# Four heads a transfer: K and V laid out 128 keys of one head to a partition, with scores, softmax and P V worked by head

## The chip, the cores and the metric

The kernel runs on one core of one Trainium2 chip. The metric is the device time of one execution in microseconds (us). Before the change the median of three runs is 98.94 us (98.93 to 99.21). The profile is of one more execution.

## What is computed

One token goes through attention and an MLP that share a normalised input. Sizes: D = 1024, 32 query heads of 128 in 4 groups (one key/value head serves 8 query heads), the last W = 4096 of 65536 cached keys, F = 3584, all in bfloat16.

```python
xn = layernorm(x)
q = (xn @ wq)                                    # 32 heads x 128
k, v = k_cache[:, :, Sk - W:, :], v_cache[:, :, Sk - W:, :]
o = softmax(q @ k.T / sqrt(128)) @ v             # each query head with its group's k, v
a = o.reshape(1, 4096) @ wo
y = layernorm(xn)
b = gelu(y @ w1 + b1) @ w2 + b2
out = x + a + b                                  # 1 x 1024
```

## The kernel before, in words

With one token every product is a vector by a matrix, so the weights and caches are read once each: W1 and W2 7 MB each, wq and wo 8 MB each, the two windows of K and V 4 MB each. Five engines run their own lists of instructions and meet at semaphores; the order is written out by hand.

**The transfers.** SP issues nearly all of them into one queue, in this order: W1 (L213), K in two transfers (`load_cache`, L204), wq (L196); when the h loop has read W1, W2 into its place (L372) and V in two transfers (L204); when the q loop has read wq, wo into its place in four chunks of 20, 8, 3 and 1 rows a partition (L196). ACT's queue brings b1, x and b2. Each K or V transfer carries two of the four heads: a partition holds 64 consecutive keys of one head, 16 KB, and even and odd partitions hold the two heads. The address of the same key in the next head is 65536 x 128 x 2 bytes further.

**The order of the work.** PE computes the sums for the two layernorms, then h = y W1 in a loop of eight turns (`rolled`, "h"). ACT copies h, PE transposes it (L397), DVE and ACT take the GELU (L402 to L418). Around that DVE turns K in 32 x 32 blocks, eight transposes of 2048 elements (`turn_k`, L331): three ahead of the GELU steps, one among them, four after. PE writes a mask of -1e30 into four PSUM banks (L429) and computes q in the loop "q", eight turns, each four column tiles abreast. q is copied (L432, L434), transposed (L438), repeated over the partition quarters (L448) and copied into LB, a zeroed array that holds q's weights at diagonal places (L457 on DVE, L458 on ACT, 128 elements each).

**Scores and softmax.** 32 matmuls of 128 x 512 (L483, through `full` and `tile`, so the profile shows L339) add into the masked banks. The mask is there because a bank holds two heads' keys alternating, and a query head must see only its own. One weight load serves two matmuls. DVE takes the maximum over each half (L487); PE transposes it (L499), DVE joins it (L502), ACT spreads it (L505), PE brings it back to the partitions (L508), and ACT makes the bias (L510) and four exponentials of 512 (L513). DVE transposes each block after its exponential (L517).

**P V and the output.** PE runs the MLP's second product in the loop "w2" (seven turns of 16 matmuls), brings the sums to the rows (L524), and runs the loop "pv": four turns of eight matmuls, 64 weights wide and 512 columns each, two column tiles abreast. A row then holds four blocks of 128, of which BLK picks the one that belongs to it: one ACT copy (L545) and three multiply-adds on DVE (L548). Four products with E4 (L557) turn this into OT, the attention vector in the form that wo needs (L564). `turn_over` (L541) is a matmul whose result nobody reads; there are one before and three after these products. The loop "wo" then takes 28 of wo's 32 rows in seven turns, each when SP has seen the chunk land (L569, L570); four rows follow outside the loop. ACT copies the result (L586), and ACT and SP store it (L589).

`rolled` is a loop on PE with addresses in registers; `Track` counts an engine's marked instructions in one semaphore.

Of the kernel before, what the change touches and what calls it, by code (L numbers as in the profile page):

```python
# [10 lines left out]
D = 1024  # L11
# [16 lines left out]
NPAIR = HKV // 2  # L28
NB = 64
OUTSIDE = -1e30  # L30
# [21 lines left out]
def bass_parallel_sum__sliding_block_cached__mixer_channel_mlp__decode_kernel(  # L52
# [26 lines left out]
    s_k = sems("s_k", NPAIR)  # L79
    s_v = sems("s_v", NPAIR)  # L80
# [14 lines left out]
    SAME = sb("SAME", [128, 128], f32)  # L95
# [3 lines left out]
    BLK = sb("BLK", [128, 4], f32)  # L99
    BLI = sb("BLI", [128, 8], f32)  # L100
    PAR = sb("PAR", [2, 128], bf16)
    OUTM = sb("OUTM", [2, 512], bf16)
    oneb = sb("oneb", [128, 32], bf16)
    XBR = sb("XBR", [1, 2 * D], bf16)
# [11 lines left out]
    LB = sb("LB", [128, 8 * 144], bf16)  # L116
# [9 lines left out]
    MXP = sb("MXP", [128, 3], f32)  # L126
    MXH = sb("MXH", [1, HQ], f32)
    MXQ = sb("MXQ", [1, 4 * HQ], f32)
    BIAS = sb("BIAS", [128, 1], f32)
    SUMS = sb("SUMS", [128, 4], f32)  # L130
    SUMP = sb("SUMP", [128, 1], f32)
# [6 lines left out]
    Pb = KV[:, 0:2048]  # L138
    PT = KV[:, 2048:4096]
# [62 lines left out]
    def load_cache(dst, cache, semaphores):  # L202
        for i in range(NPAIR):
            sp.dma_start(  # L204
                dst[:, 2 * i * W:2 * (i + 1) * W],
                cache[0, 2 * i:2 * i + 2, SK - W:SK, :].rearrange("g (m b) d -> m g (b d)", m=64),
            ).then_inc(semaphores[i], 16)

    act.dma_start(B1R, b1_row.rearrange("o (c n) -> o c n", c=B1N)).then_inc(s_b1, 16)
    act.dma_start(XBR[:, 0:D], x_row).then_inc(s_xrow, 16)  # L210
    act.dma_start(XBR[:, D:2 * D], b2_row).then_inc(s_b2, 16)

# [15 lines left out]
    def product(out, a, b, ready):  # L228
# [14 lines left out]
    POOL.mark(pool.memset(PAR[:, :], 0.0))  # L243
    fill(PAR[:, :].rearrange("k (e g r) -> k e g r", g=2, r=REP), [[0, 8], [1, 2], [0, REP]], 0, -1)
    POOL.mark(pool.memset(OUTM[:, :], OUTSIDE))
    C["mask"] = fill(OUTM[:, :].rearrange("k (s g) -> k s g", g=2), [[0, 256], [1, 2]], 0, -1, value=0.0)
    C["vec"] = POOL.mark(pool.memset(VEC[:, :], 0.0))
    POOL.mark(pool.memset(BLI[:, :], 1.0))
    fill(BLI[:, :].rearrange("p (i q) -> p i q", i=NPAIR), [[-64, NPAIR], [-16, 4]], 0, 1, op=ALU.is_ge, value=0.0)
    fill(BLI[:, :].rearrange("p (i q) -> p i q", i=NPAIR), [[64, NPAIR], [16, 4]], 15, -1, op=ALU.is_ge, value=0.0)  # L250
    pool.wait_ge(POOL.sem, POOL.cnt)
    POOL.mark(pool.tensor_tensor(out=BLK[:, :], in0=BLI[:, 0:4], in1=BLI[:, 4:8], op=ALU.add))
# [5 lines left out]
    POOL.mark(pool.tensor_tensor(out=HD[:, 0:64], in0=identf[:, 0:64], in1=identf[:, 64:128], op=ALU.add))  # L258
    pool.wait_ge(POOL.sem, POOL.cnt)
    POOL.mark(pool.tensor_tensor(  # L260
        out=SAME[:, :].rearrange("p (h b) -> p h b", b=4), in0=HD[:, 0:32].unsqueeze(2).to_broadcast([128, HQ, 4]),
        in1=HD[:, 32:64].unsqueeze(2).to_broadcast([128, HQ, 4]), op=ALU.add))
    parts = identf[:, :].rearrange("p (i q h) -> p i q h", i=NPAIR, q=4)
    POOL.mark(pool.tensor_tensor(out=HD[:, 64:128].rearrange("p (i q h) -> p i q h", i=NPAIR, q=2),
                                 in0=parts[:, :, 0:2, :], in1=parts[:, :, 2:4, :], op=ALU.add))
    pool.wait_ge(POOL.sem, POOL.cnt)
    HD4 = HD[:, 64:128].rearrange("p (i q h) -> p i q h", i=NPAIR, q=2)
    for i in range(NPAIR):
        C["consts"] = POOL.mark(pool.tensor_tensor(
            out=E4[:, :].rearrange("p (q r) -> p q r", r=129)[:, :, 64 * i:64 * i + 64:4],  # L270
            in0=HD4[:, i, 0, :].unsqueeze(1).to_broadcast([128, 4, 16]),
            in1=HD4[:, i, 1, :].unsqueeze(1).to_broadcast([128, 4, 16]), op=ALU.add))

# [52 lines left out]
    def turn_k(n):  # L326
        if n % 4 == 0:
            dve.wait_ge(s_k[n // 4], 16)
        else:
            dve.wait_ge(DVE.sem, DVE.cnt)  # L330
        C["kd"] = DVE.mark(dve.transpose(  # L331
            out=KD4[:, n], in_=KR[:, n * 2048:(n + 1) * 2048].rearrange("p (b e s) -> p b e s", b=16, e=4)))
# [47 lines left out]
    for n in range(3):  # L380
        turn_k(n)

# [26 lines left out]
    turn_k(3)  # L409
# [12 lines left out]
    for n in range(4, 8):  # L422
        turn_k(n)
# [3 lines left out]
    pe.wait_ge(POOL.sem, C["mask"])  # L427
    for n in range(4):
        tile(PS[:, n * 512:(n + 1) * 512], PAR[:, :], OUTM[:, :], (32, 128), (0, 0), n == 0, True)  # L429
# [20 lines left out]
    LB8 = LB[:, :].rearrange("p (e x) -> p e x", x=144)  # L450
    for eng, track, qs in ((dve, DVE, (0, 1)), (act, ACT, (2, 3))):
        eng.wait_ge(PE.sem, C["rep"])
        eng.wait_ge(POOL.sem, C["lb"])
        for q in qs:
            dst = LB8[32 * q:32 * q + 32, :, 32 * q:32 * q + 16]
            src = PS[32 * q:32 * q + 32, 6 * 512:6 * 512 + 128].rearrange("p (e h) -> p e h", e=8)
            C["lb", q] = track.mark(dve.tensor_copy(dst, src) if eng is dve  # L457
                                    else act.activation(out=dst, in_=src, func=ACTF.Copy))  # L458
# [19 lines left out]
    for half in range(2):  # L478
        for i in range(NPAIR):
            for e in range(4):  # L480
                for n in range(2 * half, 2 * half + 2):
                    at = (i * 4 + n) * 2048 + e * 512
                    last = full(PS[:, n * 512:(n + 1) * 512], LB[:, e * 288 + i * 128:e * 288 + i * 128 + 128],  # L483
                                KD[:, at:at + 512], n % 2 == 0)
        C["sc"] = PE.mark(last)
        dve.wait_ge(PE.sem, C["sc"])
        C["mx", half] = DVE.mark(dve.tensor_reduce(out=MXP[:, half:half + 1], in_=PS[:, half * 1024:(half + 1) * 1024], axis=AX.X, op=ALU.max))  # L487
# [4 lines left out]
    for a in range(4):  # L492
        for i in range(2):
            src = XBR[0:1, i * D + a * 256:i * D + (a + 1) * 256]
            tile(quad[a], oneb[0:1, :], src, (32, 32), (0, 32 * a), i == 0, i == 0)

    for half in range(2):
        pe.wait_ge(DVE.sem, C["mx", half])
        C["mxT"] = PE.mark(pe.matmul(PS[0:1, 6 * 512 + 256 + 128 * half:6 * 512 + 384 + 128 * half], lhsT=MXP[:, half:half + 1],  # L499
                                     rhs=identf[:, :], is_transpose=True))  # L500
    dve.wait_ge(PE.sem, C["mxT"])
    DVE.mark(dve.tensor_reduce(out=MXH[:, :], in_=PS[0:1, 6 * 512 + 256:7 * 512].rearrange("o (a h) -> o h a", a=8),  # L502
                               axis=AX.X, op=ALU.max))
    act.wait_ge(DVE.sem, DVE.cnt)
    C["mxh"] = ACT.mark(act.activation(out=MXQ[:, :].rearrange("o (q h) -> o q h", q=4),  # L505
                                       in_=MXH[:, :].unsqueeze(1).to_broadcast([1, 4, HQ]), func=ACTF.Copy))
    pe.wait_ge(ACT.sem, C["mxh"])
    C["mxb"] = PE.mark(pe.matmul(PS[:, 6 * 512 + 128:6 * 512 + 129], lhsT=MXQ[:, :], rhs=identf[0:1, 0:1]))  # L508
    act.wait_ge(PE.sem, C["mxb"])
    C["bias"] = ACT.mark(act.activation(out=BIAS[:, :], in_=PS[:, 6 * 512 + 128:6 * 512 + 129], func=ACTF.Copy, scale=-SCALE))  # L510
    act.wait_ge(ACT.sem, C["bias"])
    for n in range(4):
        C["exp"] = ACT.mark(act.activation(  # L513
            out=Pb[:, n * 512:(n + 1) * 512], in_=PS[:, n * 512:(n + 1) * 512], func=ACTF.Exp,
            bias=BIAS[:, :], scale=SCALE, accum_out=SUMS[:, n:n + 1]))
        dve.wait_ge(ACT.sem, C["exp"])
        C["tr", n] = DVE.mark(dve.transpose(  # L517
            out=PT.rearrange("p (i c h) -> p c i h", i=NPAIR, h=16)[:, 16 * n:16 * n + 16],
            in_=Pb[:, n * 512:(n + 1) * 512].rearrange("p (c i h) -> p c i h", i=NPAIR, h=16)))
    C["tot"] = DVE.mark(dve.tensor_reduce(out=SUMP[:, :], in_=SUMS[:, :], axis=AX.X, op=ALU.add))  # L520
    pe.wait_ge(s_w2, 16)
    steps("w2", W2, FC)
    pe.wait_ge(DVE.sem, C["tot"])
    C["rows"] = PE.mark(pe.matmul(PS[:, 5 * 512:5 * 512 + 1], lhsT=SAME[:, :], rhs=SUMP[:, :]))  # L524
    pe.wait_ge(DVE.sem, C["zo"])
    for sem in s_v:
        pe.wait_ge(sem, 16)

    def pv_rows(ws, vs):
        for r in range(8):  # L530
            i = r % 2
            last = tile(PS[64 * i:64 * i + 64, 4 * 512:5 * 512], vs[r], ws[r], (128, 64), (0, 64 * i))
        C["pv"] = PE.mark_loop(last, 4)

    rolled("pv", 4, (
        (lambda o: [V[:, bass.ds(o + i * 2 * W + j * 512, 512)] for j in range(4) for i in range(NPAIR)], 2048, False),
        (lambda o: [PT[:, bass.ds(o + i * 1024 + j * 64, 64)] for j in range(4) for i in range(NPAIR)], 256, True)),
# [9 lines left out]
    for c in range(1, 4):  # L547
# [3 lines left out]
        if c < 3:  # L551
# [69 lines left out]
```

## Time and profile before

| What | Number | Where |
|---|---|---|
| median of three runs | 98.94 us | the times |
| profiled execution | 99.1 us | the times |
| its span, first to last instruction | 97.8 us | the page |
| mean granted TensorE clock | 0.826 of full | the cores' view |
| bytes from HBM | 39.86 MB, 407 GB/s over the span | the page, part 3 |
| busy: PE, PEld, DVE, ACT, POOL | 48.0, 18.6, 31.7, 9.6, 10.9 us | the page, part 1 |
| scores: first matmul | 58.82 us | the timeline |
| end of the four exponentials | 73.3 us | the timeline |
| P V, 32 matmuls | 77.14 to 80.8 us | the timeline |
| first matmul of the wo loop | 88.76 us | the timeline |
| wo's last chunk lands | 95.73 us | the chain |

Times inside the execution count from the span's start. The profile's engines are PE (matmul), PEld (weight load, which overlaps PE), DVE, ACT, POOL and SP. A group of instructions is a line of the program, the engine, the operation, output and input tiles, the shape and the count, then busy time, mean and the idle time before it with what ended that idle time. "KV" is the one array that holds K as loaded, K turned, the weights P before and after their transposes, and V; "WW" holds W1, then W2, and wq, then wo; "PS" is PSUM. A transfer's time to landing counts from its issue on SP, not from its first byte.

The granted clock, in the 40 slices of the page, is full until about 32 us, half until about 54, and changes several times after.

### The profile page before, as it was taken

How to read it: one execution, taken by the hardware profiler on the slowest of the kernel's cores; microseconds unless marked ns; L12 is line 12 of the kernel's file. 1: busy time of each engine (PE TensorE's matmuls, PEld its weight loads, DVE VectorE, ACT ScalarE, POOL GpSimd, SP SyncE). 2: the span in 40 equal slices, each digit the busy share in tenths (PEclk: the TensorE clock that was granted, in tenths of full speed). 3: DMA queues.
4: the chain of work that ended last, by engine and by line, in shares of the span. 5: the costliest groups of instructions: out<-in, count | busy, mean ns of one | idle time of the engine just before them, and what ended most of it. 6: DMA issues, size and time to landing. Idle time of an engine off the chain costs nothing.

```text
span 97.8 us, 1231 instructions
## 1 busy us (share of the span) xinstructions
PE 48.0 (49%) x501; PEld 18.6 (19%) x415; DVE 31.7 (32%) x42; ACT 9.6 (10%) x23; POOL 10.9 (11%) x34
## 2 busy tenths in 40 slices
PE   0000022649720700000069939998479897926962
PEld 0000022213110000000012122121235544503530
DVE  0000003280699999994000050053282004100000
ACT  0500000140220000000000040000390001000001
POOL 2000001489980000000000000000000000000000
PEclk9999999999999555555555795899975999997599
DMA  9598888999999999999898889959999899799970
GB/s 375 234 519 375 376 375 376 415 435 429 429 569 455 482 429 509 429 429 455 382 422 375 375 375 422 610 221 429 435 429 563 352 452 486 318 415 429 394 316 1
DMA packets 1628, 39.86 MB, mean 407 GB/s; under 512 B 214, under 2 KB 218, under 8 KB 476
## 3 DMA queue, kind: packets, MB, share of 16 engines
q1 hardware_dynamic: 1588, 39.85, 95.4%
q10 hardware_dynamic: 40, 0.01, 0.1%
HBM read 39.86 MB, written 0.00 MB: 407 GB/s over the span
## 4 chain that ended last, share of the span: by engine, by line
DMA 87%; PE 7%; SPq 3%; issue 1%; ACT 0%
DMA WW<-in_A_wq_dram 48%; DMA WW<-in_A_wo_dram 39%; PE PS L339 7%; SPq L204 1%; SPq L196 1%; SPq L213 0%; ACT ORow L586 0%; SPq L375 0%
## 5 line engine op out<-in xcount | busy, mean ns | idle before, releaser
L331 DVE STREAM_TRANSPOSE KV<-KV 128x2048 bf16<-128x2048 bf16 x8 | 18.5, 2311 | 3.4 <-DMA KV<-in_A_k_cache_dram 3.2
L339 PE MATMUL PS<-WW,XNTb 128*32 x64 | 6.3, 580 | 15.4 <-SPq L375 15.4
L339 PE MATMUL PS<-WW,VEC 128*32 (+1 forms) x240 | 11.5, 345 | 4.6 <-SPq L569 3.1
L339 PE MATMUL PS<-KV,LB 128*128 128x512 bf16 x32 | 8.7, 438 | 0.7 <-DVE LB L457 0.7
L339 PEld LDWEIGHTS PS<-WW,VEC 128*32 (+1 forms) x236 | 6.1, 114 | 9.9 <-issue 8.9
L294 PE MATMUL PS<-oneb,XBR 1*128 1x1 bf16 x8 | 0.6, 194 | 14.0 <-DMA XBR<-in_A_x_dram 14.0
L339 PE MATMUL PS<-WW,YTb 128*32 x56 | 5.4, 519 | 1.5 <-DMA WW<-in_B_w_dram 1.5
L339 PEld LDWEIGHTS PS<-WW,XNTb 128*32 x32 | 1.3, 124 | 21.6 <-issue 21.6
L487 DVE TENSOR_REDUCE MXP<-PS 128x1 f32<-128x1024 f32 x2 | 2.4, 1224 | 7.6 <-PE PS L339 7.6
L297 DVE COPY XT<-PS 128x8 f32<-128x8 f32 x1 | 0.2, 167 | 14.6 <-PE PS L294 14.6
L434 DVE CAST Hs<-PS 128x512 bf16<-128x512 f32 x1 | 0.7, 692 | 11.0 <-PE PS L339 11.0
L339 PE MATMUL PS<-OUTM,PAR 2*128 2x512 bf16 x4 | 1.9, 615 | 4.4 <-DVE HT L402 4.4
L541 PE MATMUL PS<-E,identf 128*128 128x512 f32 x8 | 3.9, 616 | 0.0
L339 PE MATMUL PS<-KV 128*64 x32 | 3.6, 380 | 0.3 <-issue 0.3
L548 DVE SCALAR_TENSOR_TENSOR OD<-PS,BLK,OD 128x128 f32<-128x128 f32 x3 | 1.1, 350 | 7.3 <-ACT OD L545 7.2
L517 DVE STREAM_TRANSPOSE KV<-KV 128x512 bf16<-128x512 bf16 x4 | 2.7, 712 | 1.8 <-ACT KV L513 1.8
L294 PEld LDWEIGHTS PS<-oneb,XBR 1*128 1x128 bf16 x8 | 0.6, 159 | 13.9 <-issue 13.9
L339 PEld LDWEIGHTS PS<-KV,LB 128*128 128x128 bf16 x16 | 1.8, 111 | 7.0 <-issue 6.2
L432 ACT ACTIVATE Hs<-PS 128x512 bf16<-128x512 f32 x1 | 0.6, 597 | 23.0 <-PE PS L339 23.0
L513 ACT ACTIVATE KV<-PS,BIAS 128x512 bf16<-128x512 f32 x4 | 2.7, 685 | 0.0
L339 PEld LDWEIGHTS PS<-WW,YTb 128*32 x32 | 1.6, 112 | 5.6 <-issue 5.2
L220 POOL TENSOR_SCALAR_AFFINE_SELECT OUTM<-OUTM 2x512 bf16<-2x512 bf16 x1 | 2.3, 2302 | 0.1
(93 smaller groups left out, 37.3 us busy)
## 6 DMA issues: line engine op xcount, KB each, us to landing
WW<-in_B_w_dram SPq DMA_DIRECT2D x2, 7168.0 KB, 29.8
WW<-in_A_wo_dram SPq DMA_DIRECT2D x1, 5120.0 KB, 32.2
KV<-in_A_k_cache_dram SPq DMA_DIRECT2D x2, 2048.0 KB, 26.0
KV<-in_A_v_cache_dram SPq DMA_DIRECT2D x2, 2048.0 KB, 46.7
WW<-in_A_wo_dram SPq DMA_DIRECT2D x1, 2048.0 KB, 36.7
WW<-in_A_wo_dram SPq DMA_DIRECT2D x1, 768.0 KB, 38.1
WW<-in_A_wo_dram SPq DMA_DIRECT2D x1, 256.0 KB, 38.2
KV<-in_B_b_dram ACTq DMA_DIRECT2D x1, 7.0 KB, 9.0
```

The costliest lines, as they stand in the source:

```text
L196: sp.dma_start(dst[:, c0 * width:(c0 + n) * width].rearrange("p (c n) -> p c n", c=n), src[:, c0:c0 + n, :],).then_inc(semaphores[j], 16)
L204: sp.dma_start(dst[:, 2 * i * W:2 * (i + 1) * W], cache[0, 2 * i:2 * i + 2, SK - W:SK, :].rearrange("g (m b) d -> m g (b d)", m=64),).then ...
L220: return POOL.mark(pool.affine_select(out=out, in_=out, pattern=pattern, compare_op=op, fill=value, base=base, channel_multiplier=step))
L294: last = pe.matmul(xt[:, r:r + 1], lhsT=XBR[0:1, r:D:KC], rhs=oneb[0:1, 0:1])
L331: C["kd"] = DVE.mark(dve.transpose(out=KD4[:, n], in_=KR[:, n * 2048:(n + 1) * 2048].rearrange("p (b e s) -> p b e s", b=16, e=4)))
L339: return pe.add_instruction(mybir.InstMatmult(name=nc.get_next_instruction_name(), engine=pe.engine, ins=[lowered(rhs, False), lowered(lhs ...
L434: C["d_qs"] = DVE.mark(dve.tensor_copy(Qs[:, 512:1024], PS[:, 7 * 512:8 * 512]))
L487: C["mx", half] = DVE.mark(dve.tensor_reduce(out=MXP[:, half:half + 1], in_=PS[:, half * 1024:(half + 1) * 1024], axis=AX.X, op=ALU.max))
L513: C["exp"] = ACT.mark(act.activation(out=Pb[:, n * 512:(n + 1) * 512], in_=PS[:, n * 512:(n + 1) * 512], func=ACTF.Exp, bias=BIAS[:, :], s ...
L517: C["tr", n] = DVE.mark(dve.transpose(out=PT.rearrange("p (i c h) -> p c i h", i=NPAIR, h=16)[:, 16 * n:16 * n + 16], in_=Pb[:, n * 512:(n ...
L541: pe.matmul(PS[:, 3 * 512:4 * 512], lhsT=identf[:, :], rhs=E4[:, 0:512])
L548: C["d_od"] = DVE.mark(dve.scalar_tensor_tensor(out=OD[:, :], in0=PS[:, 4 * 512 + 128 * c:4 * 512 + 128 * c + 128], scalar=BLK[:, c:c + 1] ...
```

## The change

K and V are loaded in one transfer each. A partition now holds 128 consecutive keys of one head, 32 KB, and four neighbouring partitions hold the four heads (MB = 32 instead of m = 64). This changes what follows:

- One semaphore for K, one for V. All eight K transposes stand after the GELU steps on DVE. They write the same places.
- Scores go by head. A head's keys lie four elements (8 bytes) apart in a turned block, and 32 matmuls of 128 x 512 take them so, each with its own weights: a window of LB, which grows from 1152 to 2176 columns and takes q twice. The mask, its matmuls and its POOL instructions go.
- The maximum, its transpose, join, spread and bias are done twice, for heads 0 and 1 and for 2 and 3, and stand between the score matmuls of the later heads. Four exponentials write every fourth element.
- After the last exponential DVE transposes twice 1024 elements. Then the weights are copied four times, each time with the rows of one head kept and the others zeroed by the column GM[:, g]: the first half by four ACT copies, the second by four DVE multiplies, 512 elements each.
- The sums' weights (SUMX) are made by POOL after the exponentials.
- P V is 64 matmuls of 256 columns in eight turns, instead of 32 of 512 in four. A row holds two blocks of 128 instead of four: one multiply-add instead of three.
- One `turn_over` after the E4 products instead of three.
- b2 and x stand in two partitions of XBR, so four matmuls of K = 2 add them instead of eight of K = 1.

The core of the diff:

```diff
-NPAIR = HKV // 2
-NB = 64
+MB = 32
+NB = W // MB // 2
+WIN = 136
...
     def load_cache(dst, cache, semaphore):
-        for i in range(NPAIR):
-            sp.dma_start(
-                dst[:, 2 * i * W:2 * (i + 1) * W],
-                cache[0, 2 * i:2 * i + 2, SK - W:SK, :].rearrange("g (m b) d -> m g (b d)", m=64),
-            ).then_inc(semaphores[i], 16)
+        sp.dma_start(
+            dst[:, :], cache[0, :, SK - W:SK, :].rearrange("g (m b) d -> m g (b d)", m=MB),
+        ).then_inc(semaphore, 16)
...
     def turn_k(n):
-        if n % 4 == 0:
-            dve.wait_ge(s_k[n // 4], 16)
+        if n == 0:
+            dve.wait_ge(s_k, 16)
...
-    for n in range(3):
-        turn_k(n)
...
-    turn_k(3)
...
-    for n in range(4, 8):
+    for n in range(8):
         turn_k(n)
...
-    for n in range(4):
-        tile(PS[:, n * 512:(n + 1) * 512], PAR[:, :], OUTM[:, :], (32, 128), (0, 0), n == 0, True)
     q_rows(KC)
...
+    def scores(g):
+        for c in range(2):
             for e in range(4):
-                for n in range(2 * half, 2 * half + 2):
+                at = (e * HKV + g) * WIN + 8 - 8 * c
+                last = full(PS[:, g * 512:(g + 1) * 512], LB[:, at:at + 128],
+                            KG[:, e, g, 4 * c:4 * c + 4, :], True, c + e == 0)
...
+    scores(0)
+    scores(1)
+    take_max(0)
+    scores(2)
+    turn_max(0)
+    join_max(0)
+    scores(3)
+    take_max(1)
+    spread_max(0)
+    weigh(0)
...
+    turn_max(1)
+    join_max(1)
+    spread_max(1)
+    weigh(1)
...
+        C["tr", half] = DVE.mark(dve.transpose(out=PT[:, half * 1024:(half + 1) * 1024], in_=Pb[:, half * 1024:(half + 1) * 1024]))
+    for half, eng, track in ((0, act, ACT), (1, dve, DVE)):
+        eng.wait_ge(DVE.sem, C["tr", half])
+        for g in range(HKV):
+            dst, src = PG4[:, g, half * HB:half * HB + HB], PT4[:, half * HB:half * HB + HB]
+            C["pg", half] = track.mark(
+                dve.tensor_scalar(out=dst, in0=src, scalar1=GM[:, g:g + 1], scalar2=None, op0=ALU.mult) if half
+                else act.activation(out=dst, in_=src, func=ACTF.Copy, scale=GM[:, g:g + 1]))
     pe.wait_ge(s_w2, 16)
     steps("w2", W2, FC)
+    pool.wait_ge(ACT.sem, C["exp"])
+    C["sumx"] = POOL.mark(pool.tensor_tensor(
...
-    rolled("pv", 4, (
+    rolled("pv", NB // 8, (
+        (lambda o: [VC[:, :, bass.ds(o + r * DH, DH)] for r in range(8)], 8 * DH, False),
+        (lambda o: [PG[:, bass.ds(o + r * 64, 64)] for r in range(8)], 512, True)),
         pv_rows)
...
-    for c in range(1, 4):
+    for c in range(1, 2):
...
-    for _ in range(3):
-        turn_over()
+    turn_over()
```

## The prediction

> **What bounds the kernel now.** I read the chain that ended last first, then the transfers, then the timeline of the second half.
>
> ```profile
> DMA 87%; PE 7%; SPq 3%; issue 1%; ACT 0%
> DMA WW<-in_A_wq_dram 48%; DMA WW<-in_A_wo_dram 39%; PE PS L339 7%; SPq L204 1%; SPq L196 1%; SPq L213 0%; ACT ORow L586 0%; SPq L375 0%
> ...
> KV<-in_A_k_cache_dram SPq DMA_DIRECT2D x2, 2048.0 KB, 26.0
> KV<-in_A_v_cache_dram SPq DMA_DIRECT2D x2, 2048.0 KB, 46.7
> WW<-in_A_wo_dram SPq DMA_DIRECT2D x1, 2048.0 KB, 36.7
> WW<-in_A_wo_dram SPq DMA_DIRECT2D x1, 768.0 KB, 38.1
> WW<-in_A_wo_dram SPq DMA_DIRECT2D x1, 256.0 KB, 38.2
> ```
>
> These are parts 4 and 6 of the page (the last column is us from issue to landing). 87% of the span is one stream of transfers. All weights and both caches go through SP's queue, W1, K, wq, W2, V, wo, and each issue stands in the queue long before its turn: V is issued at 26.7 and 27.4 and lands on average 46.7 later, so the bytes ahead of it set its time, not the issue. 39.86 MB at 407 GB/s over the span leaves little idle.
>
> ```profile
> 57.44 0.04 issue
> 57.48 38.25 DMA WW<-in_A_wo_dram
> 95.73 0.04 issue
> 95.77 0.29 PE PS L339 x4
> 96.06 0.02 issue
> 96.09 0.38 ACT ORow L586
> ```
>
> This is the end of the same chain, in order of time (start, us, what). The last byte of wo lands at 95.73; only four matmuls, one copy and the two stores follow. The time is therefore the stream's end plus a fixed 2.1 us to the span's 97.8, plus 1.3 us outside it: the profiled run took 99.1, 0.16 over the median of 98.94. I forecast a difference and put it on the median.
>
> How much can the rest move before it counts? The timeline:
>
> ```profile
> 58.82 1.44 PE L339 MATMUL PS<-KV,LB 128*128 128x512 bf16 x3 [0.74 <-DVE LB L457]
> ...
> 64.06 1.22 DVE L487 TENSOR_REDUCE MXP<-PS 128x1 f32<-128x1024 f32 x1 [5.36 <-PE PS L339]
> ...
> 76.44 0.38 PE L524 MATMUL PS<-SUMP,SAME 128*128 128x1 f32 x2
> ...
> 77.14 3.65 PE L339 MATMUL PS<-KV 128*64 x32 [0.33 <-issue]
> ...
> 83.60 0.39 DVE L564 TENSOR_SCALAR VEC<-PS,REC 128x64 bf16<-128x64 f32 x1 [1.10 <-PE PS L557]
> ...
> 88.76 0.62 PE L339 MATMUL PS<-WW,VEC 128*32 x16 [2.54 <-SPq L569]
> ```
>
> The attention vector OT is done at 83.99 (83.60 + 0.39), but the wo loop starts at 88.76, released by SP when the first 20 rows of wo land. PE waits once more, 0.59 us at 93.67, again for wo. So the attention chain has 4.77 us to 88.76 and 0.59 more in the loop: about **5.3 us of cover** before a later OT moves the end.
>
> **The change, part by part.**
>
> *The stream.* The bytes stay. K becomes one issue instead of two, V likewise, and a partition's contiguous run grows from 16 KB to 32 KB. The price of a run comes from pace: the 2048 KB chunk of wo (16 KB a partition, as K and V have now) lands 4.9 us after the chunk ahead (SP was released at 88.3 and 93.2). wq, 8192 KB in 64 KB runs, takes from K's last landing to its own: issues at 1.26 and 1.92 plus twice 26.0 make 55.2 for both K landings; the first released the transposes at 25.2, so the second is at 30.0, and wq lands at 49.44. That is 19.4 us, or 4.85 per 2048 KB. K and V together, 8192 KB, can gain at most 4 x 4.9 - 19.4 = 0.2 us and, if run length does nothing, 0. Sixteen engines carry 128 rows a transfer, so K and V cost each of them 32 runs now, 16 after and would cost 8 at wq's length: 16 of 24 runs saved, 0.2 x 16/24 = **-0.13 us**. I take this. The two issues that go (0.61 to 0.69 us each in the chain's start) free SP, but SP is far ahead and nothing waits there.
>
> [...]
>
> *K's transposes.* They now wait for all of K (30.0, not 25.2) and stand behind the GELU steps on DVE. The transposes of the h row are done at 28.1; the steps on DVE and ACT are 0.22, 0.19, 0.19, 0.23, 0.14, 0.33 and 0.32 with gaps, so DVE is free at about 30. Its last step waits for POOL's constants, now at 29.1: POOL loses the mask (0.19 + 0.41 + 0.51 + 2.30) and gains about 1 us of memset of LB, so these come earlier. Then 8 x 2.34 = 18.7 us: done at 48.8. What is queued behind on DVE is the q copy at 56.1. Cover 7.3 us; cost 0. The four mask matmuls (1.9 us at 32.5) go from a stretch in which PE waits for wq: 0.
>
> *Scores.* The q copies into LB double their elements: 281 ns at 128 elements and 692 at 512 (the Hs cast) give 418, twice, +0.27 us. The scores stay 32 matmuls of 512 columns, each with its own weight load (PEld 0.1 us, beside the 0.22 us that a matmul takes where the clock is full; 16 of them already lie hidden). The keys are now read 8 bytes apart. The nearest row is the h loop's, whose operand is read in 8-byte pieces 56 bytes apart: between 24.5 and 26.3, at the full clock, 26 matmuls begin that run four abreast, so four take 1.8/6.5 = 0.28 us, the tail included; a contiguous score matmul takes 0.216. I take 0; the other end is a read at half pace, +5.2 us for the 24 that run at the full clock.
>
> *Softmax.* Two chains instead of one. By head 0 and 1: scores to 64.3, max 1.23 to 65.6, the third head's scores to 66.05, transpose, last scores to 68.1 while DVE and ACT join the max (0.41, 0.31), spread 0.38, bias 0.17, two exps of 0.67 to 70.1. By 2 and 3: max to 69.4, transpose, join, spread and bias to 71.2, exps to 72.7. Before they ended at 73.3. PE enters w2 at 71.15, 0.55 late, because it stands in the second max chain; w2 takes 5.85 as before, to 77.0.
>
> *Weights.* DVE transposes twice 1024 elements: between 712 (512) and 2311 (2048) that is 1.25 each, 72.7 to 75.2. Four ACT copies of 512 (0.60 by the Hs row) end at 76.5; four DVE multiplies lie between 0.14 (28 elements) and 0.69 (512 elements from PSUM) each: 75.8 to 78.0. w2 and the sums (0.38 + 0.7 as now) hold PE until 77.7 anyway, so P V starts at 77.7, or 78.2 at the upper end.
>
> *P V and after.* 64 matmuls of 256 columns instead of 32 of 512: the same columns, twice the weight loads and loop turns. At w2's pace (16 pairs in 0.86) 64 pairs take 3.45; at the q transposes' 78 ns a pair, 5.0; now 3.65. I take 3.8, to 81.5. Two of three multiply-adds go (350 each and a wait): OD at 82.35, four products 1.08, OT step: **OT at 83.9**, against 83.99 now. The ends of these terms: 83.5 (P V at 3.45) and 91.3 (all upper ends at once: 5.2 scores, 0.5 weights, 1.2 P V, 0.5 for strided writes and loop turns that no row prices). Two turn-overs go, 1.7 us of PE; PE then idles from 84.6 to 88.76. If this lowers the granted clock there, nothing follows: the loop's turns are 0.86 apart both where it is 0.5 (74.15, 75.02) and where it is full (70.59 to 72.38 in two).
>
> Sum: -0.13 from the stream, 0 from all that lies under it. 98.94 - 0.13 = **98.8** (the profiled time by the same sum 99.0).
>
> **The rivals.**
>
> *The attention chain outgrows its cover* (slower). Place: the strided key read in the 32 score matmuls, with the weight masks and the P V loads behind it. It decides once OT is later than 89.3, 5.3 us over now. Half pace alone (+5.2) just fits; with the upper ends of the other terms OT is at 91.3, 2.0 late, and the time 101. For it: these reads and products are in no row. Against: the h loop's pace. 0.09.
>
> *Four heads alternating slow the source* (slower). Neighbouring partitions' rows lie a head apart, 65536 x 128 x 2 B = 16 MB, now over four heads. If K and V fall to the slowest pace that a chunk shows, 768 KB in 1.9 us or 5.05 per 2048 KB, that is 4 x 0.15 = +0.6 us: 99.5. Against: two heads already alternate at full pace. 0.07.
> [...]
>
> *Merging is worth more than runs* (faster): a transfer has a cost of its own beside its runs. The 768 KB chunk lands 1.9 us after the one ahead, 0.1 above pace; if that is a cost of each transfer, two fewer give 0.2, with the full 0.2 of the runs 0.4: 98.5. Against: the 256 KB chunk is not late by as much. 0.08.
>
> **How the numbers follow.** Forecast 0.76 (own range 98.65 to 99.2, the spread of the runs shown, 98.93 to 99.21, being 0.28), slower 0.16, faster 0.08. About 0.3%, 0.3 us, is what a measurement of this kernel can tell from no change. The range takes in the source rival and the faster one, 98.5 to 99.5, and leaves the chain's 101 out.
>
> **What would show it.** Right: wo's last landing still ends the chain, near 95.6; K lands once near 30, transposes end near 49; OT between 83 and 85, and PE waits for SP before the wo loop. Wrong: PE, DVE or ACT in place of wo at the chain's end, score matmuls over 0.4 us apart at the full clock, or V landing after 76.2.

## The result and the profile after

The changed kernel takes **103.02 us** in the median of six runs (102.51 to 104.22), against 98.97 for the kernel before (98.93 to 99.21). The ratio is 1.0407, with a 95% interval of 1.0359 to 1.0455; it leaves out the longest of the six, a slow execution. The profiled execution took 102.51 us, the shortest of the six, with a span of 101.1 and a mean granted clock of 0.865. The forecast of 98.8 was wrong; the first rival, the attention chain that outgrows its cover, is what happened.

First the page of the changed kernel: the chain's shares, three groups of instructions, and the two transfers.

```profile
DMA 84%; PE 10%; issue 2%; SPq 1%; ACT 0%
...
L333 PE MATMUL PS<-KV,LB 128*128 128x512 bf16 x32 | 14.7, 630 | 1.0 <-DVE LB L445 1.0
...
L333 PE MATMUL PS<-KV 128*64 x64 | 5.0, 278 | 2.3 <-issue 1.2
...
L510 ACT ACTIVATE KV<-PS,BIAS 128x512 bf16<-128x512 f32 x4 | 5.2, 1400 | 0.1
...
KV<-in_A_k_cache_dram SPq DMA_DIRECT2D x1, 4096.0 KB, 28.7
KV<-in_A_v_cache_dram SPq DMA_DIRECT2D x1, 4096.0 KB, 49.0
```

The same groups on the page of the kernel before:

```profile
L339 PE MATMUL PS<-KV,LB 128*128 128x512 bf16 x32 | 8.7, 438 | 0.7 <-DVE LB L457 0.7
...
L513 ACT ACTIVATE KV<-PS,BIAS 128x512 bf16<-128x512 f32 x4 | 2.7, 685 | 0.0
```

The same 32 score matmuls of 512 columns were busy for 8.7 us before and are for 14.7 now. The four exponentials take 1400 ns each instead of 685. Nothing in their shapes tells why: an access pattern is not printed, only its count of elements. The two transfers are as forecast.

The end of the chain, in order of time:

```profile
55.13 37.78 DMA WW<-in_A_wo_dram
...
92.93 0.02 SPq L600
...
93.03 0.62 PE PS L333 x16
...
98.25 1.10 PE PS L333 x33
...
99.37 0.38 ACT ORow L617
```

It still names a transfer of wo, but not its last chunk: that landed at 95.44, and PE had 3.9 us left after it. The whole loop of wo stands behind 93.03. The transfer named is wo's second chunk, which was released at 92.93, by chance just as PE came to the loop; the first turn needs only the first chunk, which landed at 88.00. That it held nothing is shown by the run with 16 pairs a turn (below), where the loop starts at 91.95, before that chunk. What ended last before 93.03 is the attention vector, with one turn-over on PE beside it, which ends at 92.85; the reordered run (below) has no turn-over there and starts the loop just as long after its vector, 0.67 us against 0.68 here, so it is the vector that counts. The timeline:

```profile
57.67 11.01 PE L333 MATMUL PS<-KV,LB 128*128 128x512 bf16 x24 [0.96 <-DVE LB L445]
...
68.63 3.77 PE L333 MATMUL PS<-KV,LB 128*128 128x512 bf16 x8
...
72.44 1.23 DVE L488 TENSOR_REDUCE MXP<-PS 128x2 f32<-128x1024 f32 x1 [3.33 <-PE PS L333]
...
82.20 0.38 PE L555 MATMUL PS<-onesf,SUMX 128*128 128x1 f32 x2
...
83.67 0.63 PE L333 MATMUL PS<-KV 128*64 x8 [1.09 <-ACT KV L547]
...
84.51 0.63 PE L333 MATMUL PS<-KV 128*64 x8 [0.21 <-issue]
...
91.95 0.40 DVE L595 TENSOR_SCALAR VEC<-PS,REC 128x64 bf16<-128x64 f32 x1 [1.10 <-PE PS L589]
```

OT is done at 92.35 (91.95 + 0.40), against 83.99 before. By stretches, in us:

| Stretch | Before | After | Moves OT by |
|---|---|---|---|
| first score matmul | 58.82 | 57.67 | -1.15 |
| scores | 8.66 | 14.74 | **+6.08** |
| scores' end to w2's start | 3.12 | 3.95 | +0.83 |
| w2 | 5.91 | 5.91 | 0 |
| w2's end to P V | 0.63 | 1.40 | +0.77 |
| P V | 3.65 | 6.24 | **+2.59** |
| P V to OT | 3.20 | 2.44 | -0.76 |
| OT | 83.99 | 92.35 | +8.36 |

The first row is hardly a gain of the change: the q loop was granted a clock of 0.73 in this execution and 0.57 in that of before, and ended 1.36 earlier (0.2 of it because wq had landed sooner, 49.25 against 49.44). The second row also holds some clock: before, the first eight score matmuls ran at half the clock (0.50 granted from 59.2 to 61.9), 0.427 us apart.

### The profile page after: what moved, and what is told of

It reads as the page before. It is cut to its first block, busy times and chain, and to the rows that moved or that the text cites. A ratio compares the mean times of both kernels' runs of the same rounds, so it can differ in the third digit from the quotient of the medians.

```text
span 101.1 us, 1321 instructions
## 1 busy us (share of the span) xinstructions
PE 49.6 (49%) x523; PEld 20.5 (20%) x460; DVE 32.4 (32%) x42; ACT 15.1 (15%) x29; POOL 9.1 (9%) x33
## 4 chain that ended last, share of the span: by engine, by line
DMA 84%; PE 10%; issue 2%; SPq 1%; ACT 0%
DMA WW<-in_A_wq_dram 47%; DMA WW<-in_A_wo_dram 37%; PE PS L333 10%; SPq L203 1%; SPq L211 0%; ACT ORow L617 0%; SPq L196 0%; SPq L369 0%; SPq L600 0%
## 5 line engine op out<-in xcount | busy, mean ns | idle before, releaser
L333 PE MATMUL PS<-WW,XNTb 128*32 x64 | 5.2, 481 | 21.3 <-SPq L369 21.3
L333 PE MATMUL PS<-KV,LB 128*128 128x512 bf16 x32 | 14.7, 630 | 1.0 <-DVE LB L445 1.0
L333 PE MATMUL PS<-WW,VEC 128*32 (+1 forms) x240 | 10.2, 309 | 2.5 <-issue 2.3
L333 PE MATMUL PS<-KV 128*64 x64 | 5.0, 278 | 2.3 <-issue 1.2
L488 DVE TENSOR_REDUCE MXP<-PS 128x2 f32<-128x1024 f32 x2 | 2.4, 1224 | 10.8 <-PE PS L333 10.8
L333 PEld LDWEIGHTS PS<-KV,LB 128*128 128x128 bf16 x32 | 3.6, 116 | 10.8 <-issue 9.7
L510 ACT ACTIVATE KV<-PS,BIAS 128x512 bf16<-128x512 f32 x4 | 5.2, 1400 | 0.1
L540 DVE STREAM_TRANSPOSE KV<-KV 128x1024 bf16<-128x1024 bf16 x2 | 2.4, 1224 | 4.6 <-ACT KV L510 4.6
L333 PEld LDWEIGHTS PS<-KV 128*64 x64 | 2.9, 109 | 4.2 <-issue 4.2
L547 ACT ACTIVATE KV<-KV,GM 128x512 bf16<-128x512 bf16 x4 | 2.6, 710 | 1.3 <-DVE KV L540 1.3
```

The lines of the kernel that those rows point to most:

```text
L333: return pe.add_instruction(mybir.InstMatmult(name=nc.get_next_instruction_name(), engine=pe.engine, ins=[lowered(rhs, False), lowered(lhs ...
L488: C["mx", half] = DVE.mark(dve.tensor_reduce(out=MXP[:, 2 * half:2 * half + 2], in_=PS[:, half * 1024:(half + 1) * 1024].rearrange("p (g x ...
L510: C["exp"] = ACT.mark(act.activation(out=Pb.rearrange("p (x g) -> p g x", g=HKV)[:, g, :], in_=PS[:, g * 512:(g + 1) * 512], func=ACTF.Exp ...
L540: C["tr", half] = DVE.mark(dve.transpose(out=PT[:, half * 1024:(half + 1) * 1024], in_=Pb[:, half * 1024:(half + 1) * 1024]))
L547: else act.activation(out=dst, in_=src, func=ACTF.Copy, scale=GM[:, g:g + 1]))
```

## The experiments

The theory: keys that lie 8 bytes apart make the score matmuls slow, and exponentials that write 8 bytes apart and a P V loop with twice the turns add to it; with OT past its cover, PE's chain sets the time. The rivals: the loss is in the weight loads, which no longer serve two matmuls each; or in the transfers, with four heads alternating; or in P V alone.

**Keys contiguous.** In the changed kernel each score matmul reads 512 neighbours. These are other keys, so the scores are not the reference's.

```diff
-                            KG[:, e, g, 4 * c:4 * c + 4, :], True, c + e == 0)
+                            KD[:, ((g * 2 + c) * 4 + e) * 512:((g * 2 + c) * 4 + e) * 512 + 512], True, c + e == 0)
```

> The changed kernel, but each of the 32 score matmuls reads 512 neighbouring columns of K instead of every fourth (so the scores are of other keys than they should be); weights, their 32 loads, the number of matmuls and all else stay. Theory A, the 8-byte step of the moving operand sets the pace (0.45 us per matmul at either clock): the scores fall from 14.7 to 7-9 us, OT comes near 86, wo's landing ends the chain again, 98.6 to 98.9 us. Rival B, the weight load that every score matmul now has: scores stay at 14.7, OT at 92, time 102.5 to 104. Rival C, the order of max, join and spread between the heads' scores: the scores fall but OT does not come before 90, time over 100.

Measured: 99.2 us, ratio 0.9999 (0.9983 to 1.0014); the kernel before took 99.22 beside it. The timeline of this run:

```profile
58.32 5.35 PE L333 MATMUL PS<-KV,LB 128*128 128x512 bf16 x24 [0.96 <-DVE LB L445]
...
85.17 0.39 DVE L595 TENSOR_SCALAR VEC<-PS,REC 128x64 bf16<-128x64 f32 x1 [1.10 <-PE PS L589]
...
88.55 4.11 PE L333 MATMUL PS<-WW,VEC 128*32 x80 [2.48 <-SPq L600]
```

24 matmuls take 5.35 us instead of 11.01, each still with its own weights. OT comes at 85.56 and PE waits 2.48 us for wo: OT is inside its cover again, and the whole loss is gone, though exponentials (1.40 us) and P V (6.23) are as slow as they were.

**A load for each matmul**, in the kernel before.

```diff
-                                KD[:, at:at + 512], n % 2 == 0)
+                                KD[:, at:at + 512], True)
```

> The kernel before, with a weight load for each of the 32 score matmuls instead of each second one (the same weights again, so the same result). Theory A: the loads lie under the matmuls, scores stay at 8.7 us, time 99.0 as before. Rival B, the loads cost what the changed kernel lost: scores near 14.7 us, OT near 90, time 99.5 to 100.

Measured: ratio 1.0006 (0.9991 to 1.0021). Scores take 7.07 us, 0.216 a matmul, which is the pace at the full clock, for all 32. The 32 loads (6.60 us) lie beside the matmuls; the first rival falls.

**The stride alone**, in the kernel before: the score matmuls read every fourth element (other keys than the reference's).

```diff
-                                KD[:, at:at + 512], n % 2 == 0)
+                                KD[:, i * 8192 + e * 2048:i * 8192 + e * 2048 + 2048:4], n % 2 == 0)
```

> The kernel before, with its score matmuls reading every fourth of 2048 columns (so other keys than they should) and nothing else changed. Theory A: 32 x 0.45 = 14.5 us instead of 8.7, OT near 89.8, about half a us past its cover (84.0 + 5.8 against 89.3): ratio 1.002 to 1.012. If the cover of the prediction was too large, the ratio is over 1.02; if the matmuls' pace alone made the change slow, 1.04.

Measured: ratio 1.0192 (1.0140 to 1.0243), more than the 1.002 to 1.012 expected. Scores take 14.6 us. The timeline around OT:

```profile
88.88 2.82 PE L541 MATMUL PS<-E,identf 128*128 128x512 f32 x6
...
89.08 0.39 DVE L564 TENSOR_SCALAR VEC<-PS,REC 128x64 bf16<-128x64 f32 x1 [1.10 <-PE PS L557]
...
91.63 0.62 PE L339 MATMUL PS<-WW,VEC 128*32 x16
```

OT is done at 89.47, but the wo loop starts at 91.63: three turn-overs (six records, 2.82 us) stand ahead of it in PE's queue. In the changed kernel there is one.

**Merged transfers alone**: the kernel before with K and V in one transfer each, laid out as after the change (what lies in a row is then not what the rest of this kernel expects, so its output differs).

```diff
-        for i in range(NPAIR):
...
+        sp.dma_start(
+            dst[:, :], cache[0, :, SK - W:SK, :].rearrange("g (m b) d -> m g (b d)", m=32),
+        ).then_inc(semaphores[0], 16)
...
```

> The kernel before, with K and V in one transfer each in the changed kernel's layout (32 KB a partition, four heads alternating) and nothing else changed (so the scores and P V take rows of other heads than they should). This is the stream's term alone: forecast -0.13 us, from 0 to -0.2, ratio 0.998 to 1.000; K and V each land 0.07 us sooner after what is ahead of them. Rival, four heads alternating slow the source: K and V land later, ratio 1.006. Rival, a transfer has a cost of its own beside its runs: ratio 0.996 or less.

Measured: ratio 0.9977 (0.9954 to 1.0000), that is -0.23 us with an interval from -0.46 to 0. The landings tell it more finely. K lands 9.72 us after W1 and V 9.71 after W2; before it was 9.79 for each. In the changed kernel it is 9.74 and 9.71 (20.17 to 29.91, 66.17 to 75.88). So the merge brings each cache some 0.07 us, as forecast: four heads alternating slow nothing, and the 0.4 us of the third rival is too much. (Before, the 256 KB chunk of wo landed 0.62 us after the one ahead, at 95.73 after 95.11; at wq's 4.85 per 2048 KB it would be 0.61.) Whether the longer runs or the transfers that went bring it is not shown, since one edit changes both.

**Exponentials written contiguously**, in the changed kernel. The weights then reach P V in another order, so the output differs.

```diff
-                out=Pb.rearrange("p (x g) -> p g x", g=HKV)[:, g, :], ...
+                out=Pb[:, g * 512:(g + 1) * 512], ...
```

> The changed kernel, but each exponential writes 512 neighbouring elements instead of every fourth (so the weights stand in another order than P V takes them). Theory A2, the 8-byte step of the write doubles the exponential (1400 ns against 685): 0.69 each again; the first two stand ahead of PE's way into w2 and bring P V 1.0 us forward, the last two lie under w2: time about 102, 1.0 less than the changed kernel. Rival: the exponentials are slow for another reason (their bias by column, or contention with the transposes on DVE): they stay at 1.4 and the time at 103.

Measured: 102.24 us, ratio 1.0276 (1.0219 to 1.0332); an exponential takes 0.69 us. The step is worth 1.3% by the ratios and 0.8 us by the medians while OT sets the end; in the profiled executions the way from the first score matmul to OT is 1.63 us shorter.

**P V with 16 pairs a turn**, in the changed kernel: four turns of 16 loads and matmuls instead of eight of 8, the same matmuls.

```diff
-    rolled("pv", NB // 8, (
-        (lambda o: [VC[:, :, bass.ds(o + r * DH, DH)] for r in range(8)], 8 * DH, False),
+    rolled("pv", NB // 16, (
+        (lambda o: [VC[:, :, bass.ds(o + r * DH, DH)] for r in range(16)], 16 * DH, False),
...
```

> The changed kernel, P V in four turns of 16 matmuls instead of eight turns of 8; the same 64 matmuls and weight loads. Theory D, a turn of a PE loop costs some 0.8 us however little is in it (P V's turns are 0.78-0.83 apart with 0.43 us of columns in them, w2's 0.86 with twice as many matmuls): P V takes 3.5 to 5 us instead of 6.2 and the time falls by 1.2 to 2.6 us, ratio to before 1.015 to 1.028. Rival, the 64 weight loads of 64 columns set the pace (0.1 us each): P V stays at 6.2 and the ratio at 1.04.

Measured: 101.98 us, ratio 1.0297 (1.0246 to 1.0348). The weight loads in the timeline of this run:

```profile
84.31 0.80 PEld L333 LDWEIGHTS PS<-KV 128*64 x16 [1.68 <-issue]
...
85.48 0.80 PEld L333 LDWEIGHTS PS<-KV 128*64 x16 [0.36 <-issue]
...
86.65 0.80 PEld L333 LDWEIGHTS PS<-KV 128*64 x16 [0.37 <-issue]
```

A turn of 16 takes 1.12 to 1.17 us, one of 8 took 0.78 to 0.83. The starts of the matmuls show where this goes. Inside a turn of either kernel two matmuls, which run abreast (3 to 9 ns apart), start every 0.109 us (0.13 for the first two); their 256 columns cost that by themselves (256 x 0.42 ns, 0.216 us for 512). The rest is a gap at the end of a turn: **0.32 to 0.38 us** in turns of 8, 0.23 to 0.27 in turns of 16. In the kernel before there is none: with 512 columns a matmul, two start every 0.215 us straight through all four turns, 0.86 us of columns a turn. What PE does in the gap is not shown; in the program the loop's registers are set there.

P V takes 4.52 us instead of 6.24, but starts 0.65 later. Of this, 0.30 stands between the end of ACT's copies and the loop (1.19 us against 0.89), where the program sets twice as many registers. The run gains 1.04 us in the median, a little less than the 1.2 us that were the least expected.

**Four strides in one run.** In the changed kernel the four heads' keys are read at steps of 1, 2, 4 and 8 elements, and the exponentials write at the same steps (not the reference's data).

```diff
-                            KG[:, e, g, 4 * c:4 * c + 4, :], True, c + e == 0)
+                            KD[:, c * 8192 + e * 1024:c * 8192 + e * 1024 + 512 * 2 ** g:2 ** g], True, c + e == 0)
...
```

> The changed kernel as a gauge: the four heads' scores read K at steps of 1, 2, 4 and 8 elements (2, 4, 8, 16 bytes), and the four exponentials write at these steps (so neither the keys nor the weights are the right ones). Theory A: score matmuls 0.216 us apart at full clock at step 1, 0.45 at step 4, and the step decides, not the clock; if a line of 16 bytes is what is fetched, 0.22 at step 2 and 0.9 at step 8; if any step over one element halves the pace, 0.45 at 2, 4 and 8. The exponentials 0.69 at step 1 and 1.4 at step 4; steps 2 and 8 tell which it is there. Rival B: 0.45 at all four steps.

Measured, 512 columns: matmuls 0.216, 0.226, 0.453 and 0.900 us apart, the first three at the full clock (L478 behind them took 0.29 us, as in the changed kernel where the granted clock was 1.00). Exponentials 0.69, 0.82, 1.41 and 2.54 us. The loads of neighbouring matmuls at step 4 and at step 8, then the exponentials at 2, 4 and 8:

```profile
63.27 0.12 PEld L333 LDWEIGHTS PS<-KV,LB 128*128 128x128 bf16 x1 [0.34 <-issue]
...
63.73 0.12 PEld L333 LDWEIGHTS PS<-KV,LB 128*128 128x128 bf16 x1 [0.34 <-issue]
...
67.89 0.12 PEld L333 LDWEIGHTS PS<-KV,LB 128*128 128x128 bf16 x1 [0.78 <-issue]
...
68.79 0.12 PEld L333 LDWEIGHTS PS<-KV,LB 128*128 128x128 bf16 x1 [0.78 <-issue]
...
74.00 0.82 ACT L510 ACTIVATE KV<-PS,BIAS 128x512 bf16<-128x512 f32 x1
...
75.92 1.41 ACT L510 ACTIVATE KV<-PS,BIAS 128x512 bf16<-128x512 f32 x1
...
77.13 2.54 ACT L510 ACTIVATE KV<-PS,BIAS 128x512 bf16<-128x512 f32 x1
```

It doubles from 2 to 4 and from 4 to 8, so it goes by something that a read touches. Bytes spanned and lines of 16 bytes give the same answer up to here; wider steps tell them apart.

**Steps of 3, 6, 16 and 32** (again other data).

```diff
+                            KD[:, 0:1 + 511 * (3, 6, 16, 32)[g]:(3, 6, 16, 32)[g]], True, c + e == 0)
```

> The changed kernel as a second gauge: the four heads' score matmuls read 512 elements of K at steps of 3, 6, 16 and 32 elements (6, 12, 32, 64 bytes; other keys than they should be). If a line of 16 bytes costs 1.76 ns to fetch, as steps 2, 4 and 8 of the first gauge fit (128, 256 and 512 lines in 0.226, 0.453 and 0.90 us), the matmuls are 0.34, 0.68, 0.90 and 0.90 us apart. If the bytes spanned count instead, 0.34, 0.68, 1.8 and 3.6. If the number of elements out of order counts, the same for all four.

Measured: 0.340, 0.676, 0.917 and 0.858 us apart. From a step of 8 on it no longer grows, as lines of 16 bytes want it: every element is then in a line of its own. The clock was half at the end of step 32 (the two L483 behind it took 0.58 us together, in the changed kernel at the full clock 0.38). The price of a line does not go by the clock: the changed kernel's score matmuls are 0.453 us apart both where the granted clock was 0.50 (59.4 to 61.7) and where it was full (68.6 to 72.3). The last matmuls at step 3 were 0.427 us apart, which is the pace of 512 contiguous columns in the kernel before at half the clock.

**Pieces**: the four heads read 4 of every 8 elements, 4 of 16, 2 of 8 and 2 of 16 (other data).

```diff
+                            KD[:, 0:512 // (4, 4, 2, 2)[g] * (8, 16, 8, 16)[g]].rearrange("p (a w) -> p a w", w=(8, 16, 8, 16)[g])[:, :, 0:(4, 4, 2, 2)[g]], True, c + e == 0)
```

> The changed kernel as a third gauge: the four heads' score matmuls read 512 elements in pieces: four neighbours of each 8, four of each 16, two of each 8, two of each 16 elements (other keys than they should be). If a line of 16 bytes costs 1.76 ns, whatever lies between, the lines are 128, 128, 256 and 256 and the matmuls 0.226, 0.226, 0.453 and 0.453 us apart at the full clock; this is also why the h loop's reads of four neighbours of each 28, from which the prediction took its price, were at full pace and said nothing of single elements 8 bytes apart. If the first two are slower than 0.25, the line is not the unit and the h loop's pace has another reason.

The windows of one head each (us; busy time of PE and PEld, with counts; granted clock; share of the transfers; GB/s):

```profile
58.60:60.40 1.80, 1.80 (x9) 0.76 (x10) 1.00 1.18 510
60.40:62.20 1.80, 1.80 (x9) 0.76 (x8) 1.00 1.18 510
62.20:65.80 3.60, 3.60 (x9) 0.79 (x7) 1.00 0.91 391
65.80:69.60 3.80, 3.80 (x9) 0.92 (x8) 1.00 0.98 423
```

Eight matmuls take 1.8 us with pieces of four neighbours and 3.6 to 3.8 with pieces of two, whether the pieces lie 16 or 32 bytes apart (starts 0.226 and 0.229, then 0.452 and 0.461 us apart, all at the full clock). 512 columns touch 128 lines of 16 bytes in the first two heads and 256 in the last two. **A line costs about 1.76 ns** (0.453 / 256; 0.900 / 512), a column at the full clock 0.42 ns (0.216 / 512). Four elements a line are thus nearly hidden (1.69 ns of columns to a line) and two are not (0.84).

**Turned by head**: DVE writes the turned K so that each head's keys are neighbours, in 32 transposes of 512 elements instead of eight of 2048; the result is unchanged.

```diff
-    KD4 = KD.rearrange("p (n e b s) -> p n b e s", n=8, e=4, b=16)
+    KD4 = KD.rearrange("p (n e g b m) -> p n e b m g", n=8, e=4, g=HKV, b=16)
...
```

> The changed kernel, but DVE puts each head's keys side by side when it turns K (each of the 8 transposes cut in four by quarter of the head's width, its 32 outputs going to four places), so that the score matmuls read neighbouring columns; the result is the reference's. Theory A: scores at 0.216 us apart, OT near 87, wo's landing ends the chain, ratio 0.997 to 1.001. What can spoil it: 32 transposes of 512 at 712 ns are 22.8 us, done at 53, before q; if DVE's scattered writes double them, they end near 76, hold up the q copy behind them by 20 us and the time is near 120.

Measured: 146.39 us, ratio 1.4769, worse than the 120 that were expected at worst. The group of transposes:

```profile
L327 DVE STREAM_TRANSPOSE KV<-KV 128x512 bf16<-128x512 bf16 x32 | 74.3, 2598 | 0.2
```

The last eight score matmuls take 1.89 us, 0.216 apart again, but a transpose of 512 elements takes 2598 ns instead of 712, some 5 ns an element. 74.3 us of DVE hold up the copy of q.

**Reordered**: the changed kernel with the first maximum spread in the middle of the last head's scores, four rows of w2 taken ahead of the second maximum, 16 pairs a turn in P V and no turn-over ahead of wo; the result is unchanged.

```diff
-    scores(3)
+    scores(3, lambda: spread_max(0))
...
-    spread_max(0)
...
+    for c in range(STEP):
+        row(VEC[:, TWICE * c:TWICE * c + PAD], [W2[:, c * D + a * 256:c * D + (a + 1) * 256] for a in range(4)])
...
-    steps("w2", W2, FC)
+    steps("w2", W2, FC - STEP, c0=STEP)
...
-    turn_over()
...
```

> The changed kernel with its strided reads and writes as they are and the result unchanged, but with PE's order mended: the first max spread stands in the middle of the last head's scores (so that ACT's first two exponentials run beside them), one turn's worth of w2 stands ahead of the second max chain, P V goes 16 matmuls a turn, and the last turn-over is gone. Theory: the end is late only by what the attention chain is over its cover, so 1.7 from P V, 0.5 from the turn-over and 1.5 to 2.5 from the exponentials and w2 bring the wo loop to about 89.0-89.5: within 0.5 us of where wo's landing takes over, ratio 0.998 to 1.006. Rival, the strided reads slow more than the chain (the transfers, or the work beside them): ratio stays over 1.015.

Measured: 101.25 us, ratio 1.0213 (1.0192 to 1.0233): a miss. It is 1.9% better than the change and 2.1% worse than before, 1.77 us better in the median where 3.7 to 4.7 were expected. The ratio is over 1.015, the sign of the rival, but wo's last landing, 95.41, is where the changed kernel has it (95.44), and before it was 95.73: the strided reads of PE do not slow the transfers.

The profiled execution took 102.63, 1.4 over the median, and was granted only 0.70 of the clock in P V, so the length of P V (5.64, against 4.52 in the run with 16 pairs a turn) can't be set against the others. Three other stretches can. From the first score matmul to the end of w2 it takes 23.70 us instead of 24.60: the new order is worth 0.90, not 1.5 to 2.5. P V starts 2.07 us after w2 instead of 1.40, which takes back 0.67 of what 16 pairs a turn bring. And without the turn-over the wo loop still starts 0.67 us after OT: that term, taken as 0.5, is nothing. With the 1.72 us by which P V was shorter in that run, an estimate of the gain is 0.90 - 0.67 + 1.72 = 1.95 us, near the 1.77 measured.

## Why the prediction was wrong, step by step

**The path and its cover: right.** Here OT is set against the end of the last matmul in profiled executions:

| Kernel | Turn-overs ahead of wo | OT | Last matmul ends | Difference |
|---|---|---|---|---|
| before | 3 | 83.99 | 96.04 | waits for wo |
| keys contiguous | 1 | 85.56 | 95.82 | waits for wo |
| pieces | 1 | 89.93 | 96.96 | 7.03 |
| 16 pairs a turn | 1 | 91.28 | 98.27 | 6.99 |
| exponentials contiguous | 1 | 92.00 | 98.98 | 6.98 |
| after | 1 | 92.35 | 99.33 | 6.98 |
| reordered | 0 | 92.68 | 99.59 | 6.91 |
| steps 3 to 32 | 1 | 100.95 | 107.98 | 7.03 |
| stride alone | 3 | 89.47 | 97.83 | 8.36 |

The end is the later of the stream's (96.04) and OT + 7.0. It turns at 96.04 - 7.0 = 89.04; the prediction had 89.3, and a cover of 5.3 where it is 5.05. The changed kernel's OT is 92.35 - 89.04 = 3.31 late, and its last matmul ends 3.29 later (99.33 against 96.04). The medians are further apart, 4.05 us; what made the other executions longer than the profiled one is not shown. With three turn-overs the cover is 3.7 (96.04 - 8.36 - 83.99), so the two that went were worth 1.4 us, which the prediction counted as nothing since PE would idle there. They are nothing only while wo is late.

**Stream: right in size.** -0.13 forecast; between the landings of W1 and K and of W2 and V the changed kernel takes -0.05 and -0.08, so -0.13. That it is the length of the runs which brings this is not shown. (V's second issue is at 27.3, not 27.4 as the prediction reads it; nothing hangs on that.) Transposes of K, forecast 18.7 us and done at 48.8: done at 48.76. w2, forecast as before: 5.91 us in both.

**Scores: the step that failed.** "I take 0; the other end is a read at half pace, +5.2 us for the 24 that run at the full clock." Measured +6.08: the half pace, and 0.453 us apart at the half clock, too (0.50 granted from 59.4 to 61.7; before, 0.427 there). Against contiguous reads at the full clock all through (7.07 us, the run with a load for each) it is 7.5 to 7.7. The other end of the term, 5.2, would by itself have used up the cover of 5.05. An estimate of what the stride does alone, from its run with one turn-over counted instead of three, is an OT 89.47 - 89.04 = 0.4 us late; the rest of the 3.31 lies in the terms below. The rule of the prediction was to take the nearest row, and the h loop's row was not near. It reads pieces of 8 bytes, four neighbours in each, 56 bytes apart; the changed scores read single elements 8 bytes apart. What counts is how many lines of 16 bytes 512 columns touch: 128 in the h loop's read, 256 here (0.226 and 0.452 us in the run with pieces). The distance in bytes was compared, and the piece, which decides, was not.

**Softmax: a mis-sized term.** The exponentials were taken at 0.67 each; writing 8 bytes apart they take 1.40, and begin 1.2 apart. From the scores' end to w2 the forecast had 3.05 us (68.1 to 71.15); it took 3.95. The 0.5 us that stood "for strided writes and loop turns that no row prices" were too little.

**Weights: about right in length** (ACT's four copies 2.56 us together against 2.4; two transposes at 1.22 each against 1.25). They start late, behind the exponentials, so w2 no longer covers them: P V waited 0.77 us longer after w2 than before, the last 0.9 of its 1.40 after ACT's copies had ended. In the program the loop's registers are set behind that wait.

**P V: mis-sized, beyond its upper end.** 3.8 forecast, 5.0 at most, 6.24 measured. The columns alone take 32 x 0.109 = 3.5 us, the low end that the prediction read from w2's pace. What it left out are the gaps at the ends of turns: seven of 0.32 to 0.38 make 2.4. The row of P V before could not show them: with 512 columns a matmul its starts, 0.215 us apart, have no gap. Nor was w2's pace a price for this loop: with 16 matmuls a turn, as w2 has, a turn of P V takes 1.15 us and not 0.86.

**The chance.** The rival had 0.09, for reads and products "in no row". Its own upper ends gave 2.0 us late and 101; the range left that out, and with OT at 92.35 instead of 91.3 even they were too low. With two costs unpriced by any row and a cover that one of them nearly uses up, the two sides were nearer to even than the chances said.

No run that computes the right result beat the kernel before. That kernel with merged transfers alone measured 0.23 us less, with an interval that ends at 0, but a head's keys then lie 8 bytes apart, and the two ways tried to bring them together, the strided read and the scattered transpose, cost more.

## What to carry to other kernels

Before taking a layout that interleaves, count the lines of 16 bytes that PE's reads will touch (here 128 for 512 columns took 0.226 us, 256 took 0.453), and price strided writes by themselves (here 1.40 us for an exponential instead of 0.69): the shape in the profile doesn't show it, and a strided row of the trace is a price only for the same piece length. In a loop with addresses in registers look at the starts of matmuls inside a turn and across its end: here there was no gap with 512 columns a matmul, and one of 0.32 to 0.38 us with 256. Draw what is covered as an end time that is the later of two chains, so that costs which are hidden one by one are seen to add up once the cover is used.

## What the runs showed of the hardware that was not expected

- PE's moving operand costs a matmul about 1.76 ns for each line of 16 bytes, at the full and at the half clock (256 lines were measured at both), where its columns do not take longer: 128 lines 0.226 us, 192 (step 3) 0.340, 256 lines 0.453, 512 lines 0.858 to 0.917.
- ACT's exponentials of 512 take 0.69, 0.82, 1.41 and 2.54 us when they write at steps of 1, 2, 4 and 8 elements, from step 2 on about 4.5 ns for each 16 bytes more: (2.54 - 1.41) / 256. Whether lines or bytes spanned count here was not tested. DVE's transposes, scattered, take 5 ns an element (2598 ns for 512) instead of 1.4.
- A loop on PE with addresses in registers leaves a gap of 0.32 to 0.38 us at the end of a turn of 8 matmuls of 256 columns, and none after 8 of 512.
- Where PE's chain sets the end, the time spreads: the changed kernel's runs by 1.3 us without the longest, those of before by 0.28. The mean granted clock alone does not tell it: in the changed kernel the lower clock took longer (0.865: 102.51 us; 0.817: 103.85), in the reordered one it did not (0.829: 100.85 to 101.25; 0.849: 102.7).
